# Tokens of a store's two tiles taken in turn, eps as a small matmul for four half batches, and a new order of work

## The chip, the cores and the metric

The kernel runs on one core of a Trainium2 chip. The metric is device time in microseconds (us) for one execution. Five runs of the kernel before gave 122.39, 122.28, 122.89, 122.61 and 124.31 us: the median is 122.61. One more execution was recorded by the hardware profiler; all rows quoted below come from it.

A core has five engines that run their own instruction streams: TensorE (PE in the profile, with its weight loads listed apart as PEld), VectorE (DVE), ScalarE (ACT), GpSimd (POOL) and SyncE (SP). In this kernel SP issues every DMA transfer, in one queue and in program order. Results of TensorE land in PSUM, which has eight banks; operands live in SBUF.

## The reference, cut to what matters

There are two stages. First, linear attention with cosine weights for 8 batches, 8 heads, 576 tokens and head size 64, in float32:

```python
theta = np.pi / 2.0 * pos / S
def phi(x, c, s):
    r = np.maximum(x, 0.0)
    return np.concatenate([r * c, r * s], axis=-1)
q_p = phi(q, cos_w, sin_w); k_p = phi(k, cos_w, sin_w)
kv = np.einsum('bhsf,bhsd->bhfd', k_p, v)
z = np.sum(k_p, axis=2)
num = np.einsum('bhsf,bhfd->bhsd', q_p, kv)
den = np.einsum('bhsf,bhf->bhs', q_p, z)[..., None] + 1e-06
return (num / den)
```

Its output, with heads side by side, is x of 8 x 576 x 512. Second, a token mixer:

```python
wq = x @ w_q
wk = x @ w_k
W_tok = scale * np.einsum('bsd,btd->bst', wq, wk)
mixed = np.einsum('bst,btd->bsd', W_tok, x)
return (np.maximum(mixed, 0.0) @ w_out)
```

Here w_q and w_k are 512 x 64 and w_out is 512 x 512. The 1e-06 in `den` is the eps of this document. The kernel computes the mixer from the right: first wk' x, which is 64 x 512, and then wq times it.

## The kernel before, in words

The attention works on half batches: H = 2b + h counts 16 of them, each with four heads in two pairs j = 0, 1. A pass over one half batch has these steps, named as in the kernel (the function of that name builds the instructions):

- LD loads 288 KB of q, k or v for one pair (96 loads in all, each waiting until the buffer of half batch H - 4 has been read). LW loads w_q and w_k (`qk`) or w_out (`o`), and CW casts them to bf16.
- RK and DQ apply relu to k and q, and CV casts v to bf16. They run on ACT or POOL.
- VK (DVE, line 219) multiplies v by cosine and sine. KV (TensorE, line 236) forms kv and z, and EK copies it from PSUM.
- TQ (line 250) transposes q, and EQ (DVE, line 257) multiplies it by cosine and sine as it leaves PSUM, into the ring `qpt`. There is one EQ for each g = 2H + r.
- NM (line 271) computes the numerators and the denominators of 5 blocks of 128 tokens for one g. RC adds eps (line 286) and takes the reciprocal (line 287), both on DVE, and XN (line 292) multiplies.
- XT (line 310) transposes x, and EX copies it from PSUM.

The mixer has these steps for each batch b: WQK (line 332) and EW for wq and wk together, DW for a second copy of wq on the other half of the partitions, TK and EWK for the transposed wk, KX (line 360) and EKX for wk' x, four MX (line 379) with their EMX (relu and scaling, line 391) into `mix`, five or four WO (line 403) for output tiles of 128 tokens, each of four matmuls of 512 columns, EO that copies a tile into `osb`, and ST that stores one unit of one or two tiles. Two batches share nine tiles: `UNITS` lists the tiles of each store, `UNITS7` those of the last batch. `mix` holds the tokens of two batches in columns, and MX j = 0, 1 fill the first half of a batch's columns, 2 and 3 the second.

The program text is the long string `ORDER` (line 35). Every word names a step, the engine that takes it and, for TensorE, the PSUM bank: `WO.0.3@T2` is tile 3 of batch 0 into bank 2, `EX.5@A` a copy on ScalarE. The string is walked once, so each engine's instructions stand in the order of its own words; waits between engines are derived from what the steps read and write. Nine loads come ahead of the setup code, where 14 matmuls on a constant tile warm up TensorE, ScalarE computes the cosine tables and GpSimd builds the identity.

In the order before, the first loads are v.0.1, q.1.0, v.1.0, v.0.0, v.1.1, k.0.0, q.1.1, q.0.0 and q.0.1, so that TensorE begins with TQ.1. Counted from zero in SP's queue, LW.qk is 22nd and LW.o 37th; LD.v.13.0 is 65th and LD.v.15.0 76th, and the first store, ST.1.1, is 73rd.

Of the kernel before, what the change touches and what calls it, by code (L numbers as in the profile page):

```python
# [14 lines left out]
FP32 = mybir.dt.float32  # L15
# [9 lines left out]
N_RAW, N_RK, N_VB, N_VV, N_QD, N_QPT, N_KV = 4, 2, 2, 3, 3, 4, 3  # L25
N_XS, N_XT, N_WQK, N_WKJ, N_KX, N_MIX, N_OSB = 3, 2, 2, 2, 2, 2, 8
EPS_PE = False
XT_FULL = (0, 1, 2, 3, 4, 5, 6, 7, 8, 9, 10, 11, 12, 13, 14, 15)
UNITS = (((0, 1), (2, 3)), ((0,), (1, 2), (3, 4)))
# [6 lines left out]
LD.v.0.1@Y LD.q.1.0@Y LD.v.1.0@Y LD.v.0.0@Y LD.v.1.1@Y LD.k.0.0@Y LD.q.1.1@Y LD.q.0.0@Y  # L36
LD.q.0.1@Y DQ.1.0@A LD.k.0.1@Y CV.0.1@A LD.k.2.1@Y CV.0.0@A LD.k.1.0@Y VK.0.0@V CV.1.1@A
LD.k.1.1@Y VK.0.1@V LD.v.3.0@Y VK.1.1@V DQ.1.1@A LD.q.2.0@Y DQ.0.0@G LD.q.2.1@Y TQ.1@T0 EQ.2@V
RK.0.0@G DQ.0.1@A LD.q.3.0@Y CV.1.0@A LD.v.2.0@Y RK.0.1@G TQ.0@T2 EQ.0@V LD.q.3.1@Y KV.0@T4
EQ.1@V LD.v.2.1@Y EK.0@A EQ.3@V NM.0@T2 LD.k.2.0@Y RK.1.1@A VK.1.0@V NM.1@T4 RK.1.0@A RC.1@V  # L40
LD.k.3.1@Y XN.1@V KV.1@T0 DQ.2.0@G LW.qk@Y RC.0@V EK.1@A CV.3.0@G XN.0@V LD.v.3.1@Y NM.2@T0
RK.2.1@G NM.3@T4 DQ.3.0@A LD.q.5.0@Y RC.2@V XT.0@T2 VK.3.0@V LD.k.3.0@Y CV.2.0@G RC.3@V XN.2@V
DQ.3.1@A LD.q.5.1@Y DQ.2.1@G XN.3@V EX.0@A LD.k.4.0@Y TQ.3@T0 TQ.2@T6 VK.2.0@V XT.1@T4
LD.q.4.0@Y CV.2.1@A EQ.4@V RK.2.0@G EX.1@A LD.v.4.0@Y VK.2.1@V LD.q.4.1@Y CW.qk@G EQ.6@V KV.2@T2
RK.3.1@G EQ.5@V CV.3.1@A LD.v.4.1@Y WQK.0@T4 EK.2@A VK.3.1@V LD.v.5.1@Y NM.5@T2 EW.0@A EQ.7@V
NM.4@T6 LD.k.4.1@Y RK.3.0@G RC.4@V TK.0@T5 DW.0@G RC.5@V LD.k.5.0@Y EWK.0@A KV.3@T0 XN.5@V
DQ.5.1@A KX.0@T5 LD.v.5.0@Y RK.4.0@G EK.3@A XN.4@V EKX.0@A NM.7@T0 DQ.4.0@G LD.k.5.1@Y NM.6@T2
RC.7@V MX.0.2@T4 RC.6@V XT.2@T6 CV.4.0@G LW.o@Y EMX.0.2@A XN.7@V EX.2@A DQ.4.1@G LD.v.6.0@Y
XN.6@V DQ.5.0@G LD.k.6.0@Y TQ.4@T0 CV.4.1@A MX.0.3@T2 EQ.8@V XT.3@T4 CV.5.1@G LD.q.6.0@Y TQ.5@T6
EQ.9@V EX.3@A LD.k.6.1@Y VK.4.0@V MX.0.1@T0 LD.q.6.1@Y RK.4.1@A VK.4.1@V WQK.1@T4 EMX.0.1@A  # L50
LD.v.6.1@Y CV.5.0@G EQ.10@V EMX.0.3@A KV.4@T0 RK.5.0@G LD.q.7.0@Y EW.1@A VK.5.0@V EK.4@A TK.1@T5
RK.5.1@A VK.5.1@V NM.9@T0 MX.0.0@T2 EWK.1@A RC.9@V EMX.0.0@A KV.5@T4 XN.9@V CW.o.0@G LD.v.7.1@Y
KX.1@T3 EK.5@A EQ.11@V CW.o.1@A NM.10@T0 LD.v.7.0@Y CV.6.0@G NM.11@T4 RC.10@V LD.q.8.0@Y
RK.6.0@A WO.0.3@T2 XN.10@V DW.1@G EKX.1@A LD.k.7.1@Y DQ.6.0@A RC.11@V MX.1.0@T0 NM.8@T6 XN.11@V
EO.0.3@A LD.q.7.1@Y RK.6.1@G WO.0.0@T3 EMX.1.0@A VK.6.0@V LD.k.7.0@Y DQ.6.1@A MX.1.1@T4
MX.1.3@T0 RC.8@V WO.0.1@T2 EO.0.0@A CV.6.1@G LD.v.8.0@Y XN.8@V EMX.1.1@A WO.0.2@T3 LD.v.8.1@Y
VK.6.1@V EMX.1.3@A EO.0.1@A MX.1.2@T4 CV.7.1@G LD.q.8.1@Y TQ.6@T0 EO.0.2@A KV.6@T6 EQ.12@V
CV.7.0@G LD.k.8.0@Y EMX.1.2@A XT.5@T2 EQ.13@V EK.6@A LD.q.9.1@Y XT.4@T4 DQ.7.0@A VK.7.0@V
WO.1.4@T7 EX.5@A LD.k.8.1@Y VK.7.1@V NM.12@T0 LD.v.9.1@Y DQ.7.1@G EX.4@A WO.1.0@T6 RC.12@V
LD.q.10.1@Y RK.7.0@G XN.12@V NM.13@T2 EO.1.4@A RK.7.1@G LD.v.9.0@Y TQ.7@T4 EO.1.0@A RC.13@V  # L60
WQK.2@T0 DQ.8.0@G EQ.15@V LD.v.10.0@Y XN.13@V CV.8.1@G KV.7@T6 EW.2@A LD.q.9.0@Y CV.8.0@G
EQ.14@V DQ.8.1@A WO.1.3@T3 LD.q.10.0@Y VK.8.1@V EK.7@A TQ.8@T0 LD.k.9.1@Y EO.1.3@A VK.8.0@V
NM.15@T4 RK.8.0@A WO.1.1@T2 EQ.16@V LD.k.9.0@Y RK.8.1@G DQ.9.1@A EQ.17@V TK.2@T3 NM.14@T6
EO.1.1@A RC.15@V EWK.2@A KV.8@T0 RC.14@V DQ.10.1@G XN.15@V WO.1.2@T3 EK.8@A CV.9.1@G DW.2@A
XN.14@V XT.6@T0 CV.9.0@G EO.1.2@A VK.9.1@V NM.16@T4 LD.v.13.0@Y EX.6@A KX.2@T7 LD.k.10.0@Y
VK.9.0@V LD.k.10.1@Y XT.7@T2 DQ.9.0@G RC.16@V EKX.2@A LD.v.10.1@Y XN.16@V NM.17@T0 EX.7@A
RK.9.1@G LD.v.11.0@Y TQ.9@T6 RC.17@V LD.q.11.0@Y MX.2.2@T4 RK.9.0@G XN.17@V LD.q.11.1@Y
EMX.2.2@A MX.2.0@T2 DQ.10.0@G LD.v.11.1@Y EMX.2.0@A EQ.19@V MX.2.1@T0 ST.1.1@Y KV.9@T4 EMX.2.1@A
EQ.18@V RK.10.0@G LD.k.11.0@Y TQ.10@T2 EK.9@A MX.2.3@T0 LD.k.11.1@Y RK.10.1@G EQ.21@V WQK.3@T6
EMX.2.3@A CV.10.0@G EQ.20@V CV.10.1@A XT.8@T0 EW.3@A VK.10.0@V NM.18@T2 EX.8@A NM.19@T4  # L70
VK.10.1@V TK.3@T7 WO.2.1@T6 DW.3@G RC.19@V RC.18@V DQ.11.1@A XN.19@V WO.2.3@T1 DQ.11.0@G
# [24 lines left out]
EW.7@A EMX.6.0@A DW.7@G MX.6.1@T0 TK.7@T6 WO.6.3@T3 EMX.6.1@A EWK.7@V EO.5.3@A KX.7@T6 ST.5.2@Y
WO.6.2@T7 EKX.7@A EO.6.3@A MX.7.1@T0 EO.6.2@A MX.7.3@T2 MX.7.0@T4 WO.6.0@T6 EMX.7.0@V EMX.7.3@A
ST.6.1@Y EMX.7.1@A MX.7.2@T2 WO.6.1@T7 EMX.7.2@A EO.6.0@A WO.7.1@T5 EO.6.1@A WO.7.2@T6 ST.6.0@Y
EO.7.1@A WO.7.3@T7 EO.7.2@A WO.7.4@T5 ST.7.1@Y EO.7.3@A WO.7.0@T6 ST.7.2@Y EO.7.4@A ST.7.3@Y
EO.7.0@A ST.7.0@Y  # L100
# [4 lines left out]
def kernel(  # L105
# [28 lines left out]
    def ring(name, shape, dtype, n):  # L134
# [7 lines left out]
    qpt = ring("qpt", [P, 2, SLOTS, D], BF16, N_QPT)  # L142
    kvs = ring("kvs", [P, 2, 2, D + 2], BF16, N_KV)
    rec = ring("rec", [P, 2, SC, 1], FP32, 4)
# [6 lines left out]
    mix = ring("mix", [P, NDM, 2 * S], BF16, N_MIX)  # L151
    osb = ring("osb", [P, 2, DM], FP32, N_OSB)
    w_f = consts.tile([P, NDM, 2 * DH], FP32, name="w_f")
    wo_f = consts.tile([P, NDM, DM], FP32, name="wo_f")
    wqk_sb = consts.tile([P, NDM, 2 * DH], BF16, name="wqk_sb")
    wo_sb = consts.tile([P, NDM, DM], BF16, name="wo_sb")
    warm = consts.tile([P, 512], BF16, name="warm")
    ki = consts.tile([P, C9, 2], I32, name="ki")
    qi = vv[-1].rearrange("p r c w d -> p (r c w d)")[:, 0:4 * HC].bitcast(I32).rearrange(
        "p (w c d) -> p w c d", w=2, c=C9)  # L160
    cossin = consts.tile([P, C9, 2, D], BF16, name="cossin")
    cst = consts.tile([P, 2, C9, D], BF16, name="cst")
    ident = consts.tile([P, P], BF16, name="ident")
# [340 lines left out]
```

## Time and profile before

| what | value |
|---|---|
| median of 5 runs | 122.61 us (122.28 to 124.31) |
| the profiled execution, its own time | 122.39 us |
| its span (first to last instruction of the core) | 120.6 us |
| mean granted TensorE clock | 0.929 |
| busy TensorE / VectorE / ScalarE / GpSimd | 105.4 / 85.8 / 91.6 / 57.2 us |
| loads and stores | 39.38 MB in 20,374 packets, 326 GB/s over the span |

Busy time of TensorE counts matmuls that overlap in its pipeline; a high share is not yet full use. The profile cuts the span into 40 slices of 3.015 us and gives the busy share in tenths for each engine, the clock that the throttle granted to TensorE, and the share of time that the 16 DMA engines moved data. The chain that ended last follows the program back from its last instruction, at each step to what released it. A row of the timeline has a start, a duration, an engine and a line of the kernel, and the result and operands of the instruction; "x18" is a run of 18 instructions.

### The profile page before, as it was taken

Reading aid. Unit: us, or ns where it says so; the run is one execution under the profiler, and the core shown is the slowest. Engines: PE = TensorE matmul, PEld = TensorE weight load, DVE = VectorE, ACT = ScalarE, POOL = GpSimd, SP = SyncE. Lnnn points to the kernel's source line nnn. Section 1 sums busy time; section 2 is a strip of 40 time slices with the busy share of each in tenths; the row PEclk is TensorE's granted clock in tenths of the full one; section 3 lists DMA queues with packets and bytes.
Section 4 is the critical chain, followed back from the end, with each engine's and each line's share of the span. In section 5 each row is a group of like instructions: output and inputs, shape, how many; then the busy total and the mean of one; then the engine's idle time right before and its main releaser. Section 6 shows DMA issues by size and latency. Waiting matters only on the chain.

```text
span 120.6 us, 4909 instructions
## 1 busy us (share of the span) xinstructions
PE 105.4 (87%) x2070; PEld 66.7 (55%) x2070; DVE 85.8 (71%) x174; ACT 91.6 (76%) x155; POOL 57.2 (47%) x90
## 2 busy tenths in 40 slices
PE   5923875999688999998979999999999999999970
PEld 1303765767556637665758576565746764653420
DVE  2044989959994898999999997978899489412000
ACT  7846537637887999776999789999879763988870
POOL 6506084649668469769543945644484320020000
PEclk9995587569959999999999999999999999999999
DMA  3999999999999999994999399999999796244595
GB/s 102 364 377 407 397 394 326 383 387 394 380 396 384 386 393 388 384 355 125 344 362 360 72 346 381 375 405 406 398 404 350 289 376 238 94 175 185 214 346 215
DMA packets 20374, 39.38 MB, mean 326 GB/s; under 512 B 2944, under 2 KB 2944, under 8 KB 20352
## 3 DMA queue, kind: packets, MB, share of 16 engines
q1 hardware_dynamic: 20352, 39.07, 88.6%
q8 instruction: 16, 0.26, 0.9%
q14 instruction: 6, 0.05, 0.1%
HBM read 29.62 MB, written 9.44 MB: 324 GB/s over the span
## 4 chain that ended last, share of the span: by engine, by line
PE 41%; DMA 41%; DVE 10%; SPq 2%; ACT 2%; issue 1%; POOL 1%; POOLq 0%
PE banks L403 19%; DMA qf<-in_q_dram 14%; DMA vf<-in_v_dram 10%; DMA wo_f<-in_moe_w_out_dram 7%; DMA w_f<-in_moe_w_q_dram 6%; DMA kf<-in_k_dram 5%; PE banks L271 4%; PE banks L332 4%; PE banks L310 3%; PE banks L379 3%; PE banks L236 3%; DVE xs L292 3%; PE banks L360 3%; DVE vv L219 3%; DVE qpt L257 2%; SPq L197 2%
## 5 line engine op out<-in xcount | busy, mean ns | idle before, releaser
L403 PE MATMUL banks<-wo_sb,mix 128*128 128x512 bf16 x144 | 35.7, 381 | 0.0
L219 DVE TENSOR_TENSOR vv<-vb,cossin 128x1152 bf16<-128x1152 bf16 x32 | 26.3, 847 | 6.4 <-ACT vb L180 6.2
L292 DVE TENSOR_TENSOR xs<-banks,rec 128x640 bf16<-128x640 f32 x32 | 25.2, 810 | 0.5
L257 DVE TENSOR_TENSOR qpt<-banks,cst 128x1152 bf16<-128x1152 bf16 x32 | 22.9, 748 | 3.4 <-PE banks L250 3.1
L190 POOL TENSOR_SCALAR rk<-kf 128x576 bf16<-128x576 f32 x25 | 17.9, 720 | 11.1 <-DMA kf<-in_k_dram 9.1
L180 ACT COPY osb<-banks 128x512 f32<-128x512 f32 x36 | 20.8, 593 | 2.3 <-PE banks L403 1.7
L391 ACT ACTIVATE mix<-banks 128x576 bf16<-128x576 f32 x31 | 19.5, 661 | 2.3 <-PE banks L379 1.8
L190 POOL TENSOR_SCALAR qd<-qf 128x576 bf16<-128x576 f32 x18 | 13.2, 733 | 14.7 <-DMA qf<-in_q_dram 14.3
L403 PEld LDWEIGHTS <-mix 128*128 128x128 bf16 x144 | 12.2, 98 | 13.2 <-issue 1.1
L184 POOL TENSOR_SCALAR vb<-vf 128x576 bf16<-128x576 f32 x20 | 16.3, 819 | 5.0 <-DMA vf<-in_v_dram 1.7
L180 ACT COPY xT<-banks 128x1280 bf16<-128x1280 bf16 x13 | 15.8, 1228 | 2.2 <-PE banks L310 2.1
L271 PE MATMUL banks<-kvs,qpt 64*128 64x65 bf16 x640 | 15.0, 195 | 1.2 <-ACT kvs L180 1.2
L271 PEld LDWEIGHTS <-qpt 64*128 64x128 bf16 x640 | 12.8, 97 | 4.9 <-issue 3.3
L236 PE MATMUL banks<-vv,rk 64*64 64x131 bf16 x576 | 14.3, 243 | 0.8 <-DVE qpt L257 0.3
L236 PEld LDWEIGHTS <-rk 64*64 64x64 bf16 x576 | 11.0, 120 | 4.0 <-issue 2.6
L250 PE MATMUL banks<-ident,qd 64*128 64x64 bf16 x288 | 7.6, 202 | 5.9 <-ACT qd L188 4.0
L184 POOL TENSOR_SCALAR wq<-wqk 64x576 bf16<-64x576 bf16 x7 | 4.7, 666 | 15.6 <-ACT wqk L180 15.5
L310 PE MATMUL banks<-ident,xs 128*128 128x128 bf16 x160 | 11.8, 225 | 0.2 <-DVE xs L292 0.2
L332 PE MATMUL banks<-xT,wqk_sb 128*128 128x288 bf16 x64 | 11.1, 325 | 0.9 <-ACT xT L180 0.7
L188 ACT ACTIVATE qd<-qf 128x576 bf16<-128x576 f32 x14 | 9.6, 687 | 2.6 <-DMA qf<-in_q_dram 2.6
L310 PEld LDWEIGHTS <-xs 128*128 128x128 bf16 x160 | 9.9, 101 | 2.5 <-DVE xs L292 0.7
L180 ACT CAST kvs<-banks 128x262 bf16<-128x262 f32 x16 | 6.1, 380 | 6.1 <-PE banks L236 6.0
(42 smaller groups left out, 105.6 us busy)
## 6 DMA issues: line engine op xcount, KB each, us to landing
vf<-in_v_dram SPq DMA_DIRECT2D x32, 288.0 KB, 6.0
qf<-in_q_dram SPq DMA_DIRECT2D x32, 288.0 KB, 6.0
kf<-in_k_dram SPq DMA_DIRECT2D x32, 288.0 KB, 6.0
out_dram<-osb SPq DMA_DIRECT2D x15, 512.0 KB, 4.8
out_dram<-osb SPq DMA_DIRECT2D x6, 256.0 KB, 2.5
wo_f<-in_moe_w_out_dram SPq DMA_DIRECT2D x1, 1024.0 KB, 7.9
w_f<-in_moe_w_q_dram SPq DMA_DIRECT2D x1, 128.0 KB, 7.0
w_f<-in_moe_w_k_dram SPq DMA_DIRECT2D x1, 128.0 KB, 6.7
```

The source lines that it names most:

```text
L180: A.copy(dst, src)
L184: eng.tensor_scalar(dst, src, 1.0, 1.0, op0=ALU.mult, op1=ALU.mult)
L190: eng.tensor_scalar(dst, src, FMAX, 0.0, op0=ALU.min, op1=ALU.max)
L219: eng.tensor_mul(vv[H % N_VV][:, j, :, :, 0:D], vb[H % N_VB][:, j].unsqueeze(2).to_broadcast([P, C9, 2, D]), cossin)
L236: T.matmul(kvp[64 * j:64 * j + 64, r, :], rk[H % N_RK][64 * r:64 * r + 64, j, c, :], vv[H % N_VV][64 * r:64 * r + 64, j, c].rearrange("p w ...
L257: eng.tensor_mul(qpt[g % N_QPT][:, :, 1:SLOTS, :], qt.unsqueeze(1).to_broadcast([P, 2, C9, D]), cst)
L271: T.matmul(nv[:, j, u, :], qpt[g % N_QPT][p0:p0 + 64, w, 2 * u:2 * u + 2, :], kvs[H % N_KV][p0:p0 + 64, r, w, 0:D + 1], start=(u == 0 and ...
L292: eng.tensor_tensor(xs[b % N_XS][:, :, 4 * h + r:4 * h + r + 3:2, :].rearrange("p u h d -> p h u d"), num_view(at["NM", g])[:, :, :, 0:D], ...
L310: T.transpose(xv[:, i, u, :], x, ident)
L332: T.matmul(w[:, nh, :], wqk_sb[:, dmc, :], xT[b % N_XT][:, dmc, D + nh * HS:D + (nh + 1) * HS], start=(dmc == 0), stop=(dmc == NDM - 1))
L391: A.activation(dst, src, AF.Relu, scale=scale_moe)
L403: T.matmul(o, mix[b // 2 % N_MIX][:, dmc, base:base + P], wo_sb[:, dmc, :], start=(dmc == 0), stop=(dmc == NDM - 1))
```

## The change: what it does

**Order of tokens in a store.** In the kernel before, a tile is 128 consecutive tokens, and a store of two tiles writes two rows of 2 KB from each partition. Afterwards the two tiles of a store take the 256 tokens in turn: the first the even ones, the second the odd ones. A partition then holds two neighbouring tokens, and the store writes one row of 4 KB from it. The weight loads of these WO steps read every second column of `mix`. Stores of one tile are as before.

**eps.** For half batches 0 to 3, NM ends with two extra matmuls that add eps to the denominators (a constant tile of ones times a tile with eps split into two bf16 numbers), and RC has only the reciprocal, which reads PSUM. The other twelve half batches keep both instructions of RC.

**Buffers.** `qpt` has two tiles for a whole half batch each instead of four for one g each, and `rec` two instead of four, in the same way. The space is the same.

**Order.** The string is replaced. The same 650 steps are in it, in another order, with other banks and partly on other engines: CV 7 on ScalarE, 24 on GpSimd and 1 on VectorE (12, 20 and 0 before); RK 9 and 23 (7 and 25) and DQ 13 and 19 (14 and 18) on ScalarE and GpSimd; CW 2 and 1 (1 and 2); EK 15 on ScalarE and 1 on VectorE (16 and 0); EX 14 and 2 (13 and 3); EWK 7 and 1 (5 and 3). The nine first loads are q.0.0, q.0.1, v.0.0, k.0.0, v.0.1, k.0.1, q.1.1, v.1.1 and v.1.0. In SP's queue LW.qk is 21st and LW.o 37th; the first store, ST.1.0, is 60th, and LD.q.14.1 is 73rd. On TensorE WO.0.3 has 39 steps ahead of it instead of 37.

Further new functions and switches (steps for a whole half batch at once, wk without a transpose, a second cosine table) are defined, but the order has no such steps and the switches are off.

```diff
-N_RAW, N_RK, N_VB, N_VV, N_QD, N_QPT, N_KV = 4, 2, 2, 3, 3, 4, 3
+N_RAW, N_RK, N_VB, N_VV, N_QD, N_QPT, N_KV = 4, 2, 2, 3, 3, 2, 3
...
-EPS_PE = False
+EPS_PE = (0, 1, 2, 3)
...
 ORDER = """
-LD.v.0.1@Y LD.q.1.0@Y LD.v.1.0@Y LD.v.0.0@Y LD.v.1.1@Y LD.k.0.0@Y LD.q.1.1@Y LD.q.0.0@Y
-LD.q.0.1@Y DQ.1.0@A LD.k.0.1@Y CV.0.1@A LD.k.2.1@Y CV.0.0@A LD.k.1.0@Y VK.0.0@V CV.1.1@A
...
+LD.q.0.0@Y LD.q.0.1@Y LD.v.0.0@Y LD.k.0.0@Y LD.v.0.1@Y LD.k.0.1@Y LD.q.1.1@Y LD.v.1.1@Y
+LD.v.1.0@Y DQ.0.0@A LD.q.1.0@Y DQ.0.1@A CV.0.0@A LD.k.1.0@Y TQ.0@T0 VK.0.0@V LD.k.1.1@Y EQ.1@V
...
+EMX.0.2@A EQ.10@V CV.5.1@G LD.v.7.1@Y KV.4@T4 EW.1@A LD.k.6.1@Y RK.5.0@G MX.0.0@T0 EK.4@V
+TK.1@T7 EMX.0.0@A VK.5.1@V NM.9@T2 EWK.1@A MX.0.1@T4 NM.8@T0 RC.9@V EMX.0.1@A KV.5@T6 RC.8@V
+XN.9@V KX.1@T5 EK.5@A CW.o.0@G CW.o.1@A LD.k.7.1@Y XN.8@V NM.11@T6 NM.10@T2 LD.v.8.0@Y RC.11@V
+EKX.1@A XT.4@T0 DW.1@G RC.10@V DQ.6.0@A LD.v.7.0@Y XN.11@V WO.0.3@T5 CV.6.1@G LD.q.7.1@Y XN.10@V
...
+WO.7.4@T6 EO.7.2@A WO.7.3@T5 ST.7.1@Y EO.7.4@A WO.7.0@T7 ST.7.3@Y EO.7.3@A ST.7.2@Y EO.7.0@A
+ST.7.0@Y
...
-    qpt = ring("qpt", [P, 2, SLOTS, D], BF16, N_QPT)
+    qpt = ring("qpt", [P, 2, 2, SLOTS, D], BF16, N_QPT)
...
-    rec = ring("rec", [P, 2, SC, 1], FP32, 4)
+    rec = ring("rec", [P, 4, SC, 1], FP32, 2)
...
+    def num(H, r, nv, step, off):
         for u in range(SC):
             for w in range(2):
                 for j in range(2):
                     p0 = 64 * j
...
-                             stop=(u == SC - 1 and w == 1 and not EPS_PE))
-        if EPS_PE:
+                             stop=(u == SC - 1 and w == 1 and H not in EPS_PE))
+        if H in EPS_PE:
             for j in range(2):
                 p0 = 64 * j
-                T.matmul(nv[:, j, :, D], ones_t[p0:p0 + 64, :], eps_t[p0:p0 + 64, :],
+                T.matmul(nv[:, off + step * j, :, D], ones_t[p0:p0 + 64, :], eps_t[p0:p0 + 64, :],
                          start=False, stop=True)
+
+    def reciprocal(eng, H, dst, den):
+        if H in EPS_PE:
+            eng.reciprocal(dst, den)
+        else:
+            eng.tensor_scalar_add(dst, den, EPS)
+            eng.reciprocal(dst, dst)
...
     def WO(eng, pb, b, t):
         o = bank1(pb, 0, 4 * DM, FP32)
-        base = (t + 4 * (b % 2)) * P
+        n, ts = unit_of[b, t]
+        k = len(ts)
+        base = (ts[0] + 4 * (b % 2)) * P + ts.index(t)
         for dmc in range(NDM):
-            T.matmul(o, mix[b // 2 % N_MIX][:, dmc, base:base + P], wo_sb[:, dmc, :],
-                     start=(dmc == 0), stop=(dmc == NDM - 1))
+            T.matmul(o, mix[b // 2 % N_MIX][:, dmc, base:base + k * (P - 1) + 1:k],
+                     wo_sb[:, dmc, :], start=(dmc == 0), stop=(dmc == NDM - 1))
...
     def ST(eng, pb, b, u):
...
         dst = dataclasses.replace(
-            out, offset=out.offset + row * DM, ap=[[DM, P], [P * DM, len(ts)], [1, DM]])
-        eng.dma_start(dst, osb[n % N_OSB][:, 0:len(ts), :])
+            out, offset=out.offset + row * DM, ap=[[k * DM, P], [1, k * DM]])
+        eng.dma_start(dst, osb[n % N_OSB][:, 0:k, :].rearrange("p t n -> p (t n)"))
```

The setup code that fills the constant tiles with six memsets on GpSimd was in the kernel before already, behind a switch that was off:

```python
    if EPS_PE:
        G.memset(ones_t, 1.0)
        G.memset(eps_t, 0.0)
        for p0 in (0, 64):
            G.memset(eps_t[p0:p0 + 1, :], EPS_HI)
            G.memset(eps_t[p0 + 32:p0 + 33, :], EPS - EPS_HI)
```

## The prediction

> **What bounds the kernel now.** I read the page first (slices and chain), then the chain in order of time, then busy time by window, then single rows of the timeline. The slices of the page (3.015 us each) show three regimes:
>
> ```profile
> PE   5923875999688999998979999999999999999970
> DVE  2044989959994898999999997978899489412000
> PEclk9995587569959999999999999999999999999999
> DMA  3999999999999999994999399999999796244595
> ```
>
> DMA is full to slice 17 (54 us), with dips at slices 18 and 22. PE is at nine tenths or more from slice 13 on, but before that its granted clock falls to about half four times. The chain in order of time names the same regimes:
>
> ```profile
> 15.25 6.97 DMA w_f<-in_moe_w_q_dram
> ...
> 27.98 7.91 DMA wo_f<-in_moe_w_out_dram
> ...
> 54.64 1.41 DVE qpt L257 x2
> ...
> 111.63 5.30 PE banks L403 x24
> 116.93 0.02 issue
> 116.95 0.58 ACT osb L180
> ```
>
> Loads carry it to 54 us, VectorE to 68, TensorE from 68 to 116.93; an eviction and a store close it. By window (columns: stretch, length, busy PE, PEld, DVE, ACT, POOL, clock, DMA share, GB/s):
>
> ```profile
> 10.00:20.00 10.00, 6.56 (x203) 5.74 (x205) 7.97 (x18) 5.51 (x9) 5.69 (x8) 0.67 1.07 382
> 30.00:40.00 10.00, 8.15 (x198) 5.69 (x199) 8.24 (x14) 8.20 (x14) 7.12 (x9) 0.83 1.05 387
> 40.00:50.00 10.00, 9.98 (x190) 5.64 (x186) 9.20 (x18) 10.00 (x19) 7.38 (x9) 1.00 1.05 387
> 54.00:58.00 4.00, 3.66 (x82) 2.24 (x77) 3.93 (x10) 3.07 (x8) 3.80 (x6) 1.00 0.55 176
> 80.00:90.00 10.00, 10.00 (x228) 6.58 (x228) 8.30 (x20) 8.65 (x17) 5.77 (x9) 1.00 1.05 404
> ```
>
> Up to 40 us PE waits and runs at 0.67 to 0.83 of its clock; afterwards it is practically never idle. From 40 us to its end the windows leave only 0.02 + 0.25 + 0.34 + 0.71 + 0.21 = 1.5 us. So what counts is **how much TensorE work is behind it when the full-clock stretch begins.** The marker is the first output matmul, WO.0.3, which needs wo (landed at 35.9) and its second cast:
>
> ```profile
> 9.95 0.66 PE L250 MATMUL banks<-ident,qd 64*128 64x64 bf16 x18 [3.06 <-ACT qd L188]
> 39.24 1.05 ACT L180 CAST wo_sb<-wo_f 128x1024 bf16<-128x1024 f32 x1
> 40.26 1.04 PE L403 MATMUL banks<-wo_sb,mix 128*128 128x512 bf16 x4
> ```
>
> TensorE work at full clock, from the chain's pieces: KV 0.65, TQ 0.26, NM 0.42, XT 0.62, WQK 1.05, TK 0.15, KX 0.67, MX 0.20, WO 0.93 us (XT, WQK, TK, MX and WO are middles of several pieces). With 16, 16, 32, 16, 8, 8, 8, 32 and 36 of them the kernel has 92.8 us. The order puts 37 of them ahead of WO.0.3 (6 TQ, 6 KV, 11 NM, 4 XT, 2 WQK, 2 TK, 2 KX, 4 MX): 17.1 us. Then 40.26 + 92.8 - 17.1 = 116.0, against a true end of 116.93; the difference is the idle time. The ledger closes within 1 us.
>
> **What the Trainium skill says.** *TensorE: Matmul & The Clock Gate*, "Weight-path perf modes", says that the fast weight load takes its 32-column chunks packed or strided. No load here is strided, so the trace can't confirm it. *SBUF — State Buffer*, "Door 1: The DMA port swizzle", in its note on 16-byte cachelines, puts the free stride of bf16 at 8 elements; the new stride is 2. The same page, "two separate sides", says that a VectorE operation with two SBUF inputs and a GpSimd operation that reads SBUF lock each other out of a shared port pair. The trace agrees: the vb cast on POOL takes 0.67 us alone, 0.819 on average, and VK 0.71 to 0.76 alone, 0.847 on average. The TensorE page's Part 1 says that an idle window halves the PE clock; the row of clocks agrees.
>
> **The change, part by part.**
>
> *Start.* H0's q, v and k come first instead of a mixture of H0 and H1. In the trace the 7th load lands at 9.19 and the next ones 0.75 us apart, the first near 4.4. So the two q casts of H0 end by about 6.1 and TQ.0 can start when the warm-up ends at 6.9, not 9.95. KV.0 needs loads 3 to 6 (the last lands about 8.4) and two VK: about 9.9, against 12.14. That lead of 2 to 3 us is not kept: the first 13 loads are nearly the same set in both orders, and DVE has the same chain to pay. Walking the rows on (VK 0.75, EQ 0.75, RC + XN about 1.1) I get XN.3 at 20.1 against 20.6, and WQK.0 at about 23.3 against 23.77. NM.4 and NM.5 are then already behind it.
>
> *Weights.* The load of wq and wk moves from 22nd to 21st place in SP's queue, counted from zero: 0.75 us earlier. The load of wo stays 37th, so it lands at 35.9 again. Its second cast stays on ACT, with 34 instructions ahead instead of 36: four fewer v casts and one fewer EK, two more RK and the wqk cast, about -1.1 us. ACT is 8.2 of 10 busy there, so I count nothing.
>
> *Ahead of WO.0.3* the new order has 39 TensorE steps: the old 37 and NM.8 and XT.4. That is 0.42 + 0.62 = 1.04 us more done. XT.4 needs XN.8. DVE's first 41 steps ended at 39.79 (EQ.11); to XN.8 the new order adds RC.8 and XN.8 (1.2) and EK.4 (0.38 on ACT, taken over) and saves the eps additions. That leaves XN.8 at 39 to 40, and WO.0.3 at 40.3. **Gain 1.0 us.** If XN.8 came later, the same time would be lost again.
>
> *eps.* For H 0 to 3, eight additions of 0.151 us (plus about 0.04 between two DVE instructions) go from DVE: 1.5 us, all before 36 us, where DVE is about 82% busy. Added are 16 small matmuls with their weight loads. No row has their shape; the nearest is TQ's 64-row transpose, 18 in 0.26 us, which gives 0.2 to 0.4 us, and one exposed weight load each (0.1) would give 1.6. I take 0.3, hidden in PE's waits before 40 us; exposed, it would come on top. Six memsets on POOL (0.1 to 0.2 each, 0.7) stand behind the identity, which ended at 5.2, while POOL's next work was at 10.04 and is now due about 7: hidden.
>
> *Casts and copies between engines.* DVE takes EX.4 (0.83), EK.4 (0.38) and CV.8.0 (0.7; 0.67 on ACT, 0.757 for DVE's own 576-column copy of mix): 1.9 us. It gives up EX.11 and EX.14 (1.65), EWK.5 and EWK.6 (0.65) and the eps additions (1.5): 3.8 us. But EX.4 and CV.8.0 fall into 41 to 52 us, where DVE is over nine tenths busy and next on the chain, and most of the relief comes before or after. So I count the early saving as spent there: 0. POOL gains four v casts and a q cast for two k casts and a weight cast, about +2.7 us with the memsets at 57.2 busy: hidden by its waits, with some 0.2 us of port conflict.
>
> *SP's queue.* Two loads that stood far ahead of their turn, v.13.0 and v.15.0, held it from 50.6 to 55.3 and 62.4 to 67.5 (the DMA dips). They move back. In their place ST.1.0 comes 60th, ahead of k.9.0, and waits for EO.1.0. I put WO.1.0 at about 51, so the queue stops from 47.5 to about 52.5. About six us of loads are in flight behind an issue, so the dip is short, and PE has a backlog: by 54 us the loads landed allow 36 us of work, and 17.1 + (54 - 40.3) = 30.8 are done. Hidden; without that cover it costs up to 5 us. Later, q.14.1 and ST.2.0/ST.3.0 hold the queue, but KV.14 and KV.15 are due after 96 us: hidden.
>
> *Tokens in turn.* Each weight load of the 30 two-tile WO's, 120 of 144, reads every second bf16. Records last 98 ns and matmuls start 215 ns apart (0.86 for four), so three of four are covered even if doubled. The first of a group is exposed: 0.97 against 0.86. Bounds: 0 and 30 x 0.1 = 3.0 us. I take 0, on the two pages. The tiles 2 and 3 of an even batch and 1 and 2 of an odd one now need both halves of mix; the order already has all four MX ahead of them. In batch 7 WO.7.1 waits for the last of four EMX: up to 0.3 us.
>
> *Stores.* 15 stores of 512 KB go out in 4 KB instead of 2 KB rows: 1,920 packets fewer of 20,374. The last store has one tile and doesn't change (3.1 us from the last copy at 117.5 to the end), but what is queued ahead of it drains sooner: 0 to -0.5, I take -0.2.
>
> Sum against the profiled execution of 122.39 (120.6 span + 1.8 around it): -1.0 - 0.2 + 0 = 121.2. It stands 0.2 under the median of 122.61, so the forecast is **121.4 us**. Measurement of this kernel tells 0.5%, 0.6 us, from no change.
>
> **Rivals.**
> 1. *Lead eaten (0.22).* EX.4, EK.4 and CV.8.0 (1.9 us) make DVE late at 54 to 68, where it is on the chain, and PE waits as much as it gained. For: DVE is 3.93 of 4.00 busy there. Against: it starts earlier and is lighter by 1.9 in all. Time 122.5.
> 2. *Clock (0.13).* The half-clock stretch at 33 to 39 us goes: WQK.1 takes 1.1 instead of 2.08, KV.4 0.7 instead of 1.2. Then WO.0.3 comes 1.4 us earlier: 120.0. Against: wo's landing at 35.9 is fixed.
> 3. *Strided weights show (0.23), slower.* One mechanism: each first weight load of a two-tile WO is exposed longer, by up to 0.1 us, in a stretch where PE never waits. At +0.06 us each (1.8) the sum passes 122.61 + 0.6; at 0.1 it gives 124.4. For: nothing strided is in the trace. Against: the two pages, and cover by 215 ns matmuls.
> 4. *That it doesn't do what it says* can be seen only in part: fewer packets are certain, earlier TQ.0 nearly so.
>
> **How the numbers follow.** Main case 0.42, own range 120.4 to 122.1. Faster: main 0.37, clock 0.13, lead eaten 0.02 = 0.52. Same: main 0.05, lead eaten 0.17, strided 0.03 = 0.25. Slower: lead eaten 0.03, strided 0.20 = 0.23. The range takes the clock's gain at the low end with half a us for the store, and the full 3.0 of the weights at the top: 119.5 to 124.4.
>
> **What would show it.** TQ.0 near 6.9; eight fewer additions on DVE; WO.0.3 at 40 to 40.5 with XT.4 ahead; the four-matmul WO at 0.86 to 0.97 in the chain, and L403's weight loads still near 98 ns; DMA without a hole at 62 to 67; PE ending near 115.8. A WO of 1.05 or more, or WO.0.3 after 41.3, makes the forecast wrong.

## The result, and the profile after

The changed kernel takes 124.52 us (median of 27 runs, 122.54 to 126.68) against 123.12 us for the kernel before in the same comparisons (48 runs). The ratio is 1.0081, with a 95% interval of 1.0044 to 1.0117: **slower by 0.8%**, where 1% faster had been forecast. Executions of one kernel spread over up to 5 us here, so the ratio compares the quicker ones of both kernels (the medians of all lie 1.1% apart), and as the profiled one of the changed kernel is one of its slower ones (own time 125.31, span 123.5 us), the traces are compared stretch by stretch and not by their ends alone.

The page of the changed kernel, slices of 3.09 us:

```profile
PE   5926879688699879999797989989999999997880
...
PEclk9998555999779999999999999999999999999999
DMA  4999999999999999789999999789999852065095
```

The clock falls to half or three quarters in slices 4 to 6 and 10 to 11, less than before. What is new in the row of TensorE is above all a 7 in slice 14 (43 to 46 us) and a 7 and an 8 in slices 36 and 37 (111 to 117 us); the kernel before had 9s in all three. The row of DMA has shallow dips at 49 to 55 and 77 to 83 us (7, 8) where it had holes at slices 18 and 22; TensorE stays at 9 through the first of them. By window (columns as in the prediction: stretch, length, busy PE, PEld, DVE, ACT, POOL, clock, DMA share, GB/s):

```profile
30.00:40.00 10.00, 8.67 (x219) 6.19 (x217) 7.07 (x18) 7.54 (x13) 6.41 (x9) 0.83 1.04 388
40.00:50.00 10.00, 8.93 (x153) 4.70 (x151) 9.64 (x17) 8.17 (x15) 6.59 (x9) 1.00 1.04 380
```

Before 40 us TensorE is busier than it was (8.67 against 8.15). From 40 to 50 us, where it had 9.98, it now has 8.93, at full clock. The markers of the prediction, from the timeline:

```profile
6.24 0.44 PE L265 MATMUL banks<-ident,qd 64*128 64x64 bf16 x18
...
37.93 1.05 ACT L184 CAST wo_sb<-wo_f 128x1024 bf16<-128x1024 f32 x1
...
39.52 1.89 PE L466 MATMUL banks<-wo_sb,mix 128*128 128x512 bf16 x8
```

TQ.0 starts at 6.24 (the first transpose was at 9.95), the second cast of wo at 37.93 (39.24), and WO.0.3 at 39.52 (40.26), with two more steps done ahead of it. So the lead that was forecast is there, and more. It is lost afterwards. In the chain that ended last, the piece that used to be 24 output matmuls in one run (111.63 to 116.93) is now:

```profile
111.80 0.99 PE banks L466 x4
112.81 0.66 ACT mix L451
113.81 1.08 PE banks L466 x4
114.92 0.66 ACT mix L451
115.62 4.29 PE banks L466 x19
```

TensorE and the evictions EMX (L451) take turns at waiting for each other. The list of waits over the whole execution (total us, times, longest) has rows that have no counterpart in the kernel before, where evictions into `mix` waited for no output matmul (of the 3.6 us in the second row 2.4 are there without the turn too, in e9, as a wait for the eviction's own matmul):

```profile
ACT mix L451 <- PE banks L466: 4.0, 6, 1.0
DVE mix L453 <- PE banks L466: 3.6, 1, 3.6
PEld L466 <- ACT mix L451: 2.9, 5, 1.0
...
PE banks L466 <- ACT mix L451: 1.3, 4, 0.5
```

At its first place, in the timeline of TensorE and ScalarE:

```profile
42.41 0.82 PE L466 MATMUL banks<-wo_sb,mix 128*128 128x512 bf16 x3 [0.33 <-ACT mix L451]
...
44.73 0.65 ACT L451 ACTIVATE mix<-banks 128x576 bf16<-128x576 f32 x1 [1.03 <-PE banks L466]
...
45.43 0.72 PE L251 MATMUL banks<-vv,rk 64*64 64x131 bf16 x36 [0.74 <-ACT mix L451]
```

By the order of work, the first row is the rest of WO.0.0, which waits for EMX.1.0; the second is EMX.1.1, which waits 1.03 us for WO.0.1; the third is KV.6, whose bank EMX.1.1 has to free. But WO.0.0 and WO.0.1 read columns 0 to 255 of `mix`, and EMX.1.0 and EMX.1.1 write columns from 576 on. No data pass between them. The waits that the built program contains, traced instruction by instruction, confirm it:

```
changed kernel, eviction waits for output matmul:
  EMX.1.2 <- WO.0.0   EMX.1.1 <- WO.0.1   EMX.3.3 <- WO.2.0   EMX.6.3 <- WO.6.0
  EMX.7.0 <- WO.6.2   EMX.7.3 <- WO.6.2   EMX.7.1 <- WO.6.3
changed kernel, output matmul waits for an eviction of other columns (among others):
  WO.0.0 <- EMX.1.0   WO.0.1 <- EMX.1.2   WO.6.1 <- EMX.6.3   WO.6.3 <- EMX.7.0, EMX.7.2
kernel before, eviction waits for output matmul: none
```

The theory after this reading, W in the expectations: an eviction writes two separate runs of 288 columns, a weight load of a two-tile WO reads every second column, and the derivation of waits takes such a pair as overlapping although no element is shared. The time goes to these waits, and not to the stepped load itself.

### The profile page after: what moved, and what is told of

Same layout as the page of the kernel before. It is cut to its first block, busy times and chain, and to the rows that moved or that the text cites. A ratio compares the mean times of both kernels' runs of the same rounds, so it can differ in the third digit from the quotient of the medians.

```text
span 123.5 us, 4937 instructions
## 1 busy us (share of the span) xinstructions
PE 104.9 (85%) x2086; PEld 66.6 (54%) x2086; DVE 84.1 (68%) x163; ACT 92.3 (75%) x154; POOL 60.4 (49%) x98
## 4 chain that ended last, share of the span: by engine, by line
PE 43%; DVE 16%; DMA 16%; ACT 14%; issue 5%; SPq 3%; DVEq 0%; ACTq 0%
PE banks L466 18%; DMA qf<-in_q_dram 10%; DVE qpt L272 6%; DMA kf<-in_k_dram 5%; PE banks L292 5%; PE banks L381 5%; PE banks L251 5%; DVE xs L322 4%; DVE vv L232 4%; ACT xT L184 4%; ACT mix L451 4%; PE banks L355 4%; SPq L205 3%; PE banks L420 3%; ACT osb L184 3%
## 5 line engine op out<-in xcount | busy, mean ns | idle before, releaser
L466 PE MATMUL banks<-wo_sb,mix 128*128 128x512 bf16 x144 | 36.2, 381 | 1.3 <-ACT mix L451 1.3
L232 DVE TENSOR_TENSOR vv<-vb,cossin 128x1152 bf16<-128x1152 bf16 x32 | 27.4, 874 | 6.2 <-ACT vb L184 4.8
L451 ACT ACTIVATE mix<-banks 128x576 bf16<-128x576 f32 x31 | 19.5, 654 | 5.3 <-PE banks L466 4.0
L188 POOL TENSOR_SCALAR vb<-vf 128x576 bf16<-128x576 f32 x24 | 18.1, 758 | 10.1 <-DMA vf<-in_v_dram 6.7
L194 POOL TENSOR_SCALAR qd<-qf 128x576 bf16<-128x576 f32 x19 | 14.1, 749 | 9.3 <-DMA qf<-in_q_dram 8.9
L184 ACT COPY xT<-banks 128x1280 bf16<-128x1280 bf16 x14 | 17.0, 1232 | 1.8 <-PE banks L355 1.6
L251 PE MATMUL banks<-vv,rk 64*64 64x131 bf16 x576 | 13.6, 237 | 4.8 <-DVE qpt L272 2.0
L355 PE MATMUL banks<-ident,xs 128*128 128x128 bf16 x160 | 12.5, 231 | 0.4 <-issue 0.4
L381 PE MATMUL banks<-xT,wqk_sb 128*128 128x288 bf16 x64 | 10.3, 306 | 1.9 <-issue 0.8
L439 PE MATMUL banks<-wqk,kx 64*128 64x288 bf16 x32 | 7.6, 289 | 2.2 <-ACT xT L184 1.3
L192 ACT ACTIVATE qd<-qf 128x576 bf16<-128x576 f32 x13 | 8.8, 692 | 0.6 <-DMA qf<-in_q_dram 0.5
```

The lines of the kernel that those rows point to most:

```text
L184: A.copy(dst, src)
L188: eng.tensor_scalar(dst, src, 1.0, 1.0, op0=ALU.mult, op1=ALU.mult)
L194: eng.tensor_scalar(dst, src, FMAX, 0.0, op0=ALU.min, op1=ALU.max)
L232: eng.tensor_mul(vv[H % N_VV][:, js(j), :, :, 0:D].rearrange("p j c w d -> p (j c) w d"), vb[H % N_VB][:, js(j)].rearrange("p j c d -> p ( ...
L251: T.matmul(kvp[64 * j:64 * j + 64, r, :], rk[H % N_RK][64 * r:64 * r + 64, j, c, :], vv[H % N_VV][64 * r:64 * r + 64, j, c].rearrange("p w ...
L355: T.transpose(xv[:, i, u, :], x, ident)
```

## The experiments

All times are in us; "before" is the median of the kernel before on the same chip. The ledger has the start of the first output matmul (the marker), the end of the last, and the time between them less the TensorE work that is left behind the marker (75.7 us by the prediction's prices in the old order, 74.7 in the new). The last column is thus a remainder: besides idle time it holds work that was slower than its price, as in e4, whose clock was 0.88 from 41 to 60 us. Markers and ends are those of one traced execution each; that of e2 took 123.05 us, 3.2 more than its median.

| run | tokens in turn | eps on TensorE | median | before | ratio, 95% interval | WO.0.3 | last end | idle after |
|---|---|---|---|---|---|---|---|---|
| kernel before | no | none | 122.61 | | 1 | 40.26 | 116.91 | 1.0 |
| changed kernel | yes | H 0-3 | 124.52 | 123.12 | 1.0081 (1.0044-1.0117) | 39.52 | 119.90 | 5.7 |
| e1, the same again | yes | H 0-3 | 125.83 | 124.59 | 1.0145 (1.0069-1.0221) | 39.61 | 121.04 | 6.7 |
| e2 | no | H 0-3 | 119.81 | 124.59 | 0.9672 (0.9605-0.9740) | 38.48 | 117.57 | 4.4 |
| e9, e2 again | no | H 0-3 | 121.22 | 123.73 | 0.9843 (0.9752-0.9933) | 40.12 | 117.24 | 2.4 |
| e3 | yes, mix in pairs | H 0-3 | 121.17 | 124.59 | 0.9780 (0.9713-0.9848) | 38.72 | 115.53 | 2.1 |
| e7 | no, mix in pairs | H 0-3 | 119.81 | 123.44 | 0.9830 (0.9718-0.9943) | 38.47 | 115.93 | 2.8 |
| e4, old order | yes | none | 127.81 | 124.59 | 1.0312 (1.0238-1.0387) | 41.46 | 126.13 | 9.0 |
| e5 | no | none | 122.50 | 123.44 | 0.9938 (0.9876-1.0001) | 40.29 | 117.57 | 2.6 |
| e6, EX.14 on DVE | no | H 0-3 | 120.92 | 123.44 | 0.9811 (0.9646-0.9976) | 37.40 | 113.50 | 1.4 |
| e8, old order | no | H 0-3 | 124.41 | 123.44 | 1.0161 (1.0026-1.0295) | 40.89 | 119.06 | 2.5 |
| e10 | yes | none | 125.66 | 123.73 | 1.0202 (1.0106-1.0298) | 40.23 | 120.49 | 5.6 |
| e11 | no | H 0-5 | 121.55 | 123.73 | 0.9798 (0.9672-0.9924) | 38.28 | 113.99 | 1.0 |
| e12 | no | all H | 124.47 | 123.73 | 1.0112 (1.0020-1.0203) | 37.92 | 118.62 | 6.0 |

### The changed kernel again, and without the turn

e1 is the changed kernel unedited. e2 and e9 undo the turn of tokens alone:

```diff
-        n, ts = unit_of[b, t]
-        k = len(ts)
-        base = (ts[0] + 4 * (b % 2)) * P + ts.index(t)
+        base = (t + 4 * (b % 2)) * P
...
-            T.matmul(o, mix[b // 2 % N_MIX][:, dmc, base:base + k * (P - 1) + 1:k],
+            T.matmul(o, mix[b // 2 % N_MIX][:, dmc, base:base + P],
...
-            out, offset=out.offset + row * DM, ap=[[k * DM, P], [1, k * DM]])
+            out, offset=out.offset + row * DM, ap=[[DM, P], [P * DM, len(ts)], [1, DM]])
```

Of e1:

> The changed kernel once more, for an undisturbed profile and as the yardstick of this set. Ratio to the kernel before 1.004 to 1.012. Every theory expects WO.0.3 near 40 us with XT.4 ahead of it, and TensorE waits after 40 us of 4 to 6 us in place of 1.5 us.

Of e2:

> The changed kernel with the tiles of a store as they were before (consecutive tokens, 2 KB rows, contiguous weight loads); order and eps as changed. Theory W (the strided reads bring extra waits between the evictions EMX and the output matmuls WO, in both directions, and these cost the time): 2 to 3 us faster than the changed kernel, ratio to the kernel before 0.985 to 0.995, and no EMX that waits for a WO. Theory O (the new order itself loses it, by ScalarE's queue): ratio stays at 1.004 to 1.012.

Of e9:

> The changed kernel with tokens not in turn once more, on the chip of the next three. Theory D (in the new order VectorE works without a break from 11 us to XN.8, so each eps addition that is gone brings WO.0.3 forward; after WO.0.3 TensorE has 74.7 us of work and 1 to 3 us of idle time): WO.0.3 at 37.8 to 38.6 us, time 119.2 to 120.9 us. Theory R (the 119.8 us was the luck of one chip): 121.5 us or more, not to be told from the 122.5 us of the order alone.

Measured: 125.83 with the turn and 119.81 without it on one chip, 121.22 without it on another. e1 has the early marker and the idle time that were expected, at a ratio a little above its range (1.0145 against 1.012 at most). **The new order with eps is faster than the kernel before by 1.6 to 3.3%; the turn more than takes that away.** Theory W had the direction right, but forecast 2 to 3 us and a ratio of 0.985 to 0.995: e2 is 6.0 us faster at 0.967, e9 just beyond the range at 0.984. Theory R falls in so far as e9 too is faster than the kernel before (its interval ends at 0.9933); but the 3.3% of e2 did not come again, and e9 can't be told from the order alone (e5 below). Theory D missed for e9: 121.22 lies above its range, and WO.0.3 came at 40.12, not below 38.6.

That slow start of e9 makes it a good partner for the changed kernel: both traces reach the marker about together, and evictions into `mix` can be set against their counterparts. Starts of some of them, from the trace of ScalarE (where a row of the timeline holds several, each has its own start here):

| eviction | changed kernel | e9, no turn | difference |
|---|---|---|---|
| EMX.1.0 | 41.71 | 42.31 | -0.60 |
| EMX.1.1 | 44.73 | 43.87 | +0.86 |
| EMX.2.2 | 59.92 | 59.16 | +0.76 |
| EMX.2.3 | 63.66 | 65.10 | -1.44 |
| EMX.3.3 | 78.01 | 77.46 | +0.55 |
| EMX.5.3 | 97.21 | 96.63 | +0.58 |
| EMX.6.1 | 105.99 | 105.40 | +0.59 |
| EMX.6.3 | 109.73 | 108.58 | +1.15 |
| EMX.7.3 | 112.81 | 110.80 | +2.01 |
| EMX.7.1 | 114.92 | 112.00 | +2.92 |
| last output matmul ends | 119.90 | 117.24 | +2.66 |

The changed kernel loses 1.5 us between 41 and 45 us and 2.1 us from 106 us on, at just the places of the waits that join batches 0 and 1 and batches 6 and 7. Between them the two traces drift apart and together again: e9 stops for 1.2 us near 61 us and has a clock of 0.83 from 60 to 70 us, and the changed kernel loses its lead of 1.44 us again by EMX.3.3, which waits 0.50 us for WO.2.0.

The other traces of the new order tell the places of the turn from this drift. Counted from its own marker, EMX.1.1 starts after 5.21 us in all three traces with the waits (the changed kernel, e1 and e10) and after 3.74 in all seven without them (e2, e3, e5, e6, e7, e9 and e11, among them e3, which keeps the turn). From the start of EMX.6.1 to the end of the last output matmul it is 13.91 us in each of the three and 11.79 to 11.91 in the seven. **So the waits cost 1.5 and 2.1 us, 3.5 in all, in every trace that has them.** The stretch between the two places takes 61.1 to 62.3 us in the three and 60.1 to 63.6 in the seven, so the turn doesn't show there. (e12 is left aside, as it has more matmuls.) In e9 the same instructions of ScalarE and TensorE stand at these places without a gap:

```profile
43.32 1.21 ACT L451 ACTIVATE mix<-banks 128x576 bf16<-128x576 f32 x2
...
44.73 0.72 PE L251 MATMUL banks<-vv,rk 64*64 64x131 bf16 x36
...
110.80 1.85 ACT L451 ACTIVATE mix<-banks 128x576 bf16<-128x576 f32 x3
...
111.89 5.35 PE L464 MATMUL banks<-wo_sb,mix 128*128 128x512 bf16 x24
```

Three evictions in one run and 24 matmuls in one run replace the alternation that the chain of the changed kernel shows.

### Keep the turn, take away what makes the waits

e3 keeps tokens in turn, 4 KB rows and the order. It only lays `mix` out so that the two channels of an eviction lie side by side: the eviction writes one unbroken run, and the weight loads step by four elements (two in one-tile stores).

```diff
-    mix = ring("mix", [P, NDM, 2 * S], BF16, N_MIX)
+    mix = ring("mix", [P, 2, 2 * S, 2], BF16, N_MIX)
...
-        dst = mix[b // 2 % N_MIX].rearrange("p (r i) n -> p r i n", r=2)[
-            :, :, i, o:o + NT].rearrange("p r (d c) -> p r d c", c=C9)
+        dst = mix[b // 2 % N_MIX][:, i, o:o + NT, :].rearrange("p (d c) r -> p d c r", c=C9)
...
-            T.matmul(o, mix[b // 2 % N_MIX][:, dmc, base:base + k * (P - 1) + 1:k],
+            T.matmul(o, mix[b // 2 % N_MIX][:, dmc % 2, base:base + k * (P - 1) + 1:k, dmc // 2],
```

> The changed kernel with tokens still taken in turn and 4 KB rows, but with mix laid out so that one eviction writes one unbroken run (the two rows r of a token next to each other); weight loads then step by 4 elements, or by 2 for a store of one tile. The extra waits between EMX and WO are gone, the strided weight load stays. Theory W: as fast as the run with consecutive tokens within 0.5%, if the eviction stays at 0.65 us. Theory S (the strided weight load itself is slow): no faster than the changed kernel, WO over 0.97 us. Theory O: ratio stays at 1.004 to 1.012.

e7 has the same layout without the turn: all 144 weight loads step by two, and no tile of a store needs the columns of its neighbour.

> The changed kernel with mix laid out in pairs, so that its evictions write one unbroken run and the weight loads of the output matmuls read every second column (all 144 of them), but tokens not in turn: stores in 2 KB rows, each tile of 128 neighbouring tokens. Theory W (the waits between disjoint evictions and tiles cost the time, stepped loads by themselves nothing): 119.8 us as without the turn, output matmuls at 380 to 385 ns, weight loads at 98 ns. Theory S (every stepped weight load costs up to 0.1 us where it is exposed): 36 tiles by 0.03 to 0.1 us, so 121 to 123.4 us, output matmuls above 400 ns.

Measured: 121.17 for e3 against 125.83 for the changed kernel on the same chip, and 119.81 for e7. The built program of e3 has no wait of an eviction for an output matmul, and its list of waits has for the evictions on ScalarE only this row, for their own matmuls:

```profile
ACT mix L450 <- PE banks L439: 0.4, 2, 0.2
```

At the first of the two places e3 has, 3.20 us after its marker of 38.72, two evictions in one run, as e9 has:

```profile
41.92 1.21 ACT L450 ACTIVATE mix<-banks 128x576 bf16<-128x576 f32 x2
```

**So the waits cost the time; what the turn costs besides is small.** Theory W forecast e3 within 0.5% of e2. On the same chip it is 1.1% slower (121.17 and 119.81, intervals of the ratios overlapping), and against e9, on another chip, 0.6% faster by the ratios; a cost of the turn itself of up to 1.4 us is not excluded. The stepped load of two elements has no part in it: before the change (first row) a load takes 98 ns, in the changed kernel (second row, steps of two in 120 of 144) as well, and no load there takes over 102 ns. Steps of four in e3 (third row) do take longer, 113 ns on average with the 24 that step by two, and output matmuls are at 382 ns instead of 381:

```profile
L403 PEld LDWEIGHTS <-mix 128*128 128x128 bf16 x144 | 12.2, 98 | 13.2 <-issue 1.1
```

```profile
L466 PEld LDWEIGHTS <-mix 128*128 128x128 bf16 x144 | 12.4, 98 | 15.8 <-ACT mix L451 2.9
```

```profile
L465 PEld LDWEIGHTS <-mix 128*128 128x128 bf16 x144 | 14.1, 113 | 12.5 <-issue 1.7
```

In e7, with all loads stepped by two, they take 98 ns too. The real dependence of a pair on both halves of `mix`, and the rows of 4 KB, distinguish e3 from e7, and so does the step of four; their ratios (0.978 and 0.983) can't be told apart, so none of these shows in the time.

### The turn on the old order

e4 is the kernel before with the new WO and ST (the reverse of the diff of e2). WO.6.3 stands ahead of EMX.6.1 in the old order, so one tile of batch 6 is computed from columns that are not yet written; no step is left out.

> The kernel before with only the tokens taken in turn (stores of 4 KB rows, strided weight loads). Theory W: nine evictions now wait for an output matmul of another column range, 1.5 to 3 us slower, ratio 1.012 to 1.025. Theory P (larger rows help the queue): 0.3 to 1 us faster. If the loss belongs to the new order alone: ratio 0.997 to 1.003.

Measured 127.81, 3.1% slower (2.4 to 3.9%), more than the 1.2 to 2.5% of theory W. The same kinds of waits appear, and more of them (list of waits):

```profile
ACT mix L391 <- PE banks L405: 7.3, 9, 1.7
DVE mix L393 <- PE banks L405: 4.3, 1, 4.3
```

So the turn costs time on both orders: 3.1% on the old one, 2.4 to 4.7% on the new one (with the spread of the experiments above).

### What the order and eps are worth

e5 is e2 without the eps matmuls, e10 the changed kernel without them, e8 the kernel before with them; e11 and e12 are e2 with them in six and all sixteen half batches. Each changes one line as this one does (e8 also the three places that then have to ask for the half batch):

```diff
-EPS_PE = (0, 1, 2, 3)
+EPS_PE = ()
```

Of e5:

> The changed kernel with tokens not in turn (as before the change) and without the eps matmuls: only the new order is left. Theory M (the order brings the gain by itself, eps is a detail): within 0.7 us of the 119.8 us that the kernel without the turn took, that is 119.5 to 120.6 us, since only eight additions (1.5 us of VectorE, all before 36 us) come back. Theory E (the order depends on the relief of VectorE before 36 us, and without it WO.0.3 comes later by as much): 121 to 122 us, WO.0.3 a microsecond or more after 40 us.

Of e8:

> The kernel before with the eps matmuls for half batches 0 to 3 only; order, stores and buffers as before. Theory M (eps is hidden relief of VectorE): within 0.5% of the kernel before, at most 0.6 us faster. Theory E (eps on TensorE moves the start of the full-clock stretch): 1 us or more faster, with WO.0.3 at 39.3 us or earlier instead of 40.26.

Of e10:

> The changed kernel as it is, with tokens in turn, but with no eps matmuls: all sixteen half batches keep the addition. Theory D with theory W: both costs stand side by side, 1.5 to 2.5 us for the additions and 5 to 6 us for the turn, so 126 to 128 us. If the waits that the turn brings swallow what the additions cost (TensorE waits for ScalarE after 42 us anyway), 124.5 to 125.8 us, as the changed kernel.

Of e11:

> Tokens not in turn, and eps on TensorE for six half batches instead of four: half batches 4 and 5 lose their four additions, whose two pairs stood at 34.3 and 36.7 us in the trace of the run with EX.14 on VectorE. Theory D: the first pair is ahead of XN.8 and brings WO.0.3 forward by 0.3 to 0.5 us, so 0.3 to 0.8 us faster than without the turn. If TensorE or ScalarE is the one that sets WO.0.3: no change.

Of e12:

> Tokens not in turn, and eps on TensorE for all sixteen half batches. Twenty-four more pairs of 64x5 matmuls stand in the stretch from 40 us on, in which TensorE never waits; a pair takes 0.17 to 0.18 us in the rows of the trace but the next group of matmuls starts 0.03 us after it. Theory D: 24 x 0.03 to 0.10 us = 0.7 to 2.4 us of TensorE work more, VectorE lighter by 24 x 0.15 us where it no longer counts: 120 to 122 us. If the relief of VectorE up to 68 us counts too, 118.5 to 119.5 us.

The order alone (e5) gives 0.6%, just within what could be nothing. With eps it gives 1.6 to 3.3%. On the old order eps brings no gain (e8, if anything 1.6% slower), and with the turn its absence costs about 1% (e10 is 1.2% above the changed kernel and 0.6% above e1 by the ratios, intervals overlapping), as the second of e10's theories has it. Without eps the turn costs 2.6% (e10 against e5). The forecasts for e5 and e8 came out in neither of their theories: e5 is slower than both ranges, with WO.0.3 only 0.3 us after 40, and e8 is slower instead of equal or faster; why is open. One pair of RC on VectorE, first of e5, where additions stand ahead of the reciprocals, then of e6, where eps is in the sum already (rows of the timeline):

```profile
12.79 0.16 DVE L306 TENSOR_SCALAR rec<-banks 128x10 f32<-128x10 f32 x1
12.99 0.22 DVE L307 RECIPROCAL rec<-rec 128x10 f32<-128x10 f32 x1
...
13.39 1.49 DVE L322 TENSOR_TENSOR xs<-banks,rec 128x640 bf16<-128x640 f32 x2
```

```profile
13.06 0.28 DVE L304 RECIPROCAL rec<-banks 128x10 f32<-128x10 f32 x2
13.30 1.56 DVE L322 TENSOR_TENSOR xs<-banks,rec 128x640 bf16<-128x640 f32 x2
```

From the first RC to XN it is 0.60 us in one and 0.24 in the other. Between 20 and 30 us VectorE is 9.01 (e5) and 9.29 (e6) of 10 busy, so there is little slack to hide them. WO.0.3 starts at 40.23 and 40.29 in the two runs of the new order without eps, and between 37.40 and 40.12 in the seven traces with eps on H 0 to 3, on average at 38.9. That is what 1.5 us of additions on the way to it would do, but the spread is as large, and one trace of each is all there is. What eps is worth in the new order is left open between nothing and 2 us: measured beside e5 (0.9938), e6 and e7, which have eps but one more edit each, stand at 0.981 and 0.983, with intervals that overlap.

e11 shows no gain over e9 (0.9798 against 0.9843, with wide intervals). e12 loses: 1.1% slower than before. Its marker is early (37.92) but 6.0 us are idle or new behind it, so more than the 0.7 to 2.4 us that were expected for 24 pairs of small matmuls. One stop of 1.79 us for XN at 70 us is part of it; the rest stays open.

### EX.14 back on VectorE

In the changed kernel ScalarE has EX.15 and EX.14 in a row near 105 us. e6 is e2 with one word of the order changed:

```diff
-... EX.15@A ST.5.0@Y WO.5.3@T7 EX.14@A WO.5.1@T6 ...
+... EX.15@A ST.5.0@Y WO.5.3@T7 EX.14@V WO.5.1@T6 ...
```

> The changed kernel with tokens not in turn and EX.14 on VectorE, as the kernel before had it (one word of the order). Theory M: in the tail ScalarE has two copies of x in a row (EX.15 and EX.14, 2.35 us together) while VectorE is nearly idle; if TensorE waits for EX.14, this saves up to 1 us: 118.8 to 119.8 us. If WQK.7 has other work of TensorE in front of it that hides the copy, 119.8 us, no change.

Median 120.92, between e2 and e9: no difference that these runs can tell. Its profiled run was the quickest seen, 118.97 us, and shows the best that the new order did: a clock of 1.00 from 20 to 38 us, where the kernel before had 0.67 and 0.79, WO.0.3 at 37.40, and a remainder of 1.4 us afterwards. That the clock alone brings WO.0.3 so far forward is not shown: e7 has 1.00 there as well, and WO.0.3 at 38.47.

**The version that beats both kernels** is the changed one without the turn: 119.81 and 121.22 us (e2, e9), with e3, e6, e7 and e11 in the same range.

## Why the prediction was wrong, point by point

The forecast was 121.4 us, with a range of 119.5 to 124.4; the result is 124.52. The kernel before was at 122.61 where the forecast began and at 123.12 beside the changed kernel, so on the forecast's scale the ratio makes 123.6: by either number on the other side of no change.

- **Start: right.** TQ.0 at 6.24 (6.9 forecast), KV.0 from 8.70 (9.9). WQK.0 at 22.72 (23.3).
- **Weights: direction right, then discarded.** The second cast of wo was reckoned 1.1 us earlier and counted as nothing. It came 1.3 us earlier in the changed kernel (37.93), and up to 3.4 in e6.
- **Ahead of WO.0.3: right, and too small.** 39 steps were done, XT.4 among them, but at 39.52 and not 40.3: a lead of 1.8 us instead of 1.0. Without the turn it is 1.2 to 3.9 us (1.04 plus 40.26 less the marker).
- **eps: costs right, value unsettled.** A pair of small matmuls takes 0.17 to 0.23 us in the rows and is hidden before 40 us. The counting of the relief as nothing neither stands nor falls.
- **Casts and copies: 0 can stand.** No run took these moves apart; e6 for EX.14 found no difference.
- **SP's queue: hidden, as said.** The stop forecast for 47.5 to 52.5 us fits the dip of the DMA row at 49 to 55, and TensorE has work through it; in e6 there is no dip at all (393 GB/s from 50 to 60 us).
- **Tokens in turn: the step that failed.** It asked what a stepped load costs and took 0. For the step of two that was right: the Trainium skill, *TensorE: Matmul & The Clock Gate*, "Weight-path perf modes", lets the fast weight load read its chunks strided, and the 98 ns agree. The free stride of 8 elements of bf16 that the prediction took from the skill's *SBUF — State Buffer*, "Door 1: The DMA port swizzle", doesn't hold for these loads at a step of four, where e3 has 116 ns on average; there the measurement decides. It also asked which evictions a tile's data need ("the order already has all four MX ahead of them", true as well). It did not ask which further waits would be derived from the new access patterns, and so put them at nothing. They cost 3.5 us in each trace that has them, and by the ratios the turn costs between 2.4% (the changed kernel's 1.0081 less e9's 0.9843) and 4.7% (e1 less e2). "WO.7.1 waits for the last of four EMX: up to 0.3" was the right kind of thing in the one place where it is real; measured there: 0.53, with EMX.7.1 itself late by the 0.91 us that it waits for WO.6.3.
- **The ledger.** The forecast passed the marker's gain on to the end whole, and so left the 1.0 us behind the marker as it was. It became 5.7 us, 4.7 more (39.52 + 74.7 + 5.7 = 119.9). Counted by windows, TensorE is busy for 75.12 of the 76.65 us from the marker to the last output matmul before, and for 74.91 of 80.38 us after: 1.5 and 5.5 us idle. The waits of the turn are 3.5 us of the 5.7; the rest is not assigned to a cause.
- **Stores: nothing.** From the last output matmul to the end of the span it is 3.6 us (3.7 before).
- **The signs.** Of the two that were to make the forecast wrong, WO.0.3 after 41.3 did not come, and a WO of 1.05 or more only in one of two pieces of the chain (0.99 and 1.08). The sign that told was the end of TensorE, 119.90 instead of 115.8. A slip in reading without weight for the sum: TensorE was not at nine tenths or more in all slices from 13 on (in the kernel before, slices 18 and 20 have 8 and 7).

The rivals: strided weights ended on the right side by luck, since its mechanism did not happen: no weight load of the changed kernel takes over 102 ns. The clock's gain (120.0) is near the times of the runs without the turn, and half-clock time from 30 to 38 us is gone or nearly gone in them (1.00 in e2, e3, e6 and e7, 0.93 in e9); but it is gone in e1 and e10 too (1.00), which have the turn and take 125.8 and 125.7 us, so the clock is not what separates them. "Lead eaten" was true, but in the main not by VectorE: from 54 to 68 us TensorE waits for it for 1.6 us in the changed kernel's trace, 0.7 in the kernel before and 0.5 in e1.

Three things stay open. That the derivation of waits takes a two-run write and a stepped read as overlapping is inferred from three layouts (both together: waits; either alone: none), not read in its code. It is not shown why the ratios for the turn spread from 2.4 to 4.7% while the waits cost the same 3.5 us in each trace. And what eps is worth is not settled.

## What to carry to other kernels

A new access pattern changes not only what an instruction costs but which waits the program gets. Before a stepped or interleaved view goes into a kernel whose waits are derived, compare the list of waits of the built programs, and look for pairs that share no element; a layout that makes one side an unbroken run can remove them. And keep a ledger of marker, work left and idle time: it shows at once whether a gain was never made or was made and lost later.

## What the runs showed of the hardware that was not expected

- Weight loads of 128 columns: 98 ns at a step of one or two bf16 elements; in e3 98 ns for the 24 that step by two, and 111 to 138, on average 116, for the 120 that step by four. Output matmuls take 380 to 382 ns with all three steps on the new order.
- Stores of 512 KB landed (median of a trace) after 4.1 (the changed kernel) to 5.0 us (e10) with rows of 4 KB, and after 4.1 (e2, e9) to 5.2 us (e11) with rows of 2 KB: the size of the row doesn't show, and the 1,920 packets fewer bring no time that shows.
- Before 40 us nearly the same instructions reach the same marker at 37.40 to 40.12 us (e2, e6, e7, e9), with mean clocks from 20 to 30 us of 0.90, 1.00, 1.00 and 0.71. When half-clock stretches fall differs from one execution to the next. In these four the lowest clock goes with the latest marker; how much of the spread of the times comes from it is not shown.
